# A first stage with an opening written out for three pairs, V in four loads, and inverse sums and weights at other steps

## The chip, the cores and the metric

The kernel runs on one core of one Trainium2 chip. The metric is the device time of one execution in microseconds (us). The engines are TensorE (PE), VectorE (DVE), ScalarE (ACT), GpSimd (POOL) and SyncE (SP), which here issues nearly all DMA transfers.

## What is computed

Attention over 4 batches, 12 heads, 448 positions and 64 columns per head, then two dense layers with gates. The reference, cut:

```python
def rmsnorm(x, g):
    return x / np.sqrt(np.mean(x * x, axis=-1, keepdims=True) + 1e-06) * g
q_n, k_n = rmsnorm(q, g_q), rmsnorm(k, g_k)
scores = np.matmul(q_n, k_n.transpose(0, 1, 3, 2)) / np.sqrt(64)
scores = scores - np.max(scores, axis=-1, keepdims=True)
attn = np.exp(scores)
attn = attn / (np.sum(attn, axis=-1, keepdims=True) + 1e-09)
x = np.matmul(attn, v)                 # then to (1792, 768)
g = x @ w_gate                         # 768 x 1536
x = (g / (1 + np.exp(-g)) * (x @ w_val)) @ w_out
h = x @ w2_in                          # 768 x 2048
out = (h * np.cos(h)) @ w2_out         # (1792, 768)
```

## The kernel before

Two heads of a batch make a pair; there are 24 pairs, six to a batch, and 7 column blocks (`NS`) to a pair. The kernel has a first stage for the 12 pairs of batches 0 and 1 (`NC`), a second for the attention of batches 2 and 3 beside the first dense layers, and stages for the remaining dense layers. The change touches the first stage.

The first stage is a loop over steps `n`, 7 steps to a pair. A table of offsets (`OFF`, third entry, less `CSH` = 12) says at which step each part of a pair's preparation is written: the loads of k and q into `rqk` (35 steps ahead of the pair's step 0), squares on ACT (L349) and their sums on VectorE (`ss`, L350), a power on POOL that gives the inverse norms (`ri`, from `ss` and `half`), products of k with the gains (L363) and of k and q with `ri` (k on VectorE, L408; q on POOL), casts to f16 on ACT (L423, L437) and the low halves on POOL (`h16`, L429 and L443), and a DMA transpose of `h16` into `T` (`c_T`, 18 steps ahead). The loop runs from step -35 on, and all of this goes through the table.

Of a pair's `T`, VectorE makes two copies (`c_copy`, L666 and L667) and ACT one, into the constant tile `cC`. `c_s` (12 steps ahead) makes scores on TensorE and takes each block's row maxima on VectorE (`sm`, L680). `c_row` puts the 7 maxima into the constant tile `cw` (L687, L688) and has TensorE turn them into rows by 7 small matmuls (`s<-id,cw`). `c_st` then makes transposed scores less their maxima, with `T` and `cC` as weights, and ACT's exponential (`pr`, L713). `c_av` multiplies with V: the tile `cV` holds V of a head beside ones, so that the same matmul gives outputs and sums. `c_x` copies the outputs out (`co`, L741). The sums go by DMA into a small tile (`c_sum`, `sm<-co`), are inverted (`c_inv`, L752, L753), written to DRAM (`c_out`, `rc<-sm`) and read back over 64 partitions each (`c_back`, `cr<-rc`); `c_mul` multiplies (L774), `c_lo` makes a low half. `CEND` holds the steps of these seven behind `c_x`. `v_max`, `v_row` and `v_out` find the largest element of V of a batch for a scale: two loads of V, two reductions, a matmul with the identity, small rows on VectorE, and a second matmul.

The constants of `cC`, `cw` and `cV` are set once per buffer by `c_const` on POOL (three buffers, the second and third at steps `CC1` and `CC2`).

Weights come as 64-bit numbers. `WSTEP` says at which steps of the first stage a piece is loaded (`raw`), converted to f32 by three rows on VectorE (L936 to L938) and squared on ACT, and split in two f16 halves (L968 on ACT, L969 on VectorE) that are also stored to DRAM (`scr_...`).

In this stage SP's and POOL's instructions stay in the order in which the code is written; TensorE's do so from step 75 (`EARLY`) on. For the others a scheduler sets the order when the kernel is built. Every engine runs its own list in order, so a row that waits holds all behind it. Operations on SP, POOL and TensorE pass a helper and have its line, L163.

Of the kernel before, what the change touches and what calls it, by code (L numbers as in the profile page):

```python
# [9 lines left out]
F32 = mybir.dt.float32  # L10
# [17 lines left out]
VM0 = 22  # L28
VM1 = 2
# [8 lines left out]
CXL = 11  # L38
VM2 = 46
CC1 = 22  # L40
CC2 = 29
# [8 lines left out]
for _u in range(WAHEAD):  # L50
    for _d, _w in ((-6, ("load", 0)), (-3, ("load", 1)), (0, ("conv", 0)), (4, ("conv", 1)), (7, ("scale", 1)), (8, ("split", 0)), (12, ("split", 1))):
        WSTEP.setdefault(8 + 16 * _u + _d, []).append((_w[0], 2 * _u + _w[1]))
# [119 lines left out]
def kernel(ctx: ExitStack, tc, q, k, v, g_q, g_k, w_gate, w_val, w_out, w2_in, w2_out, out):  # L172
# [84 lines left out]
    def emit_consts(gtmp):  # L257
        sync.dma_start(gk, g_k.partition_broadcast(P))
        sync.dma_start(gtmp, g_q.partition_broadcast(P))
        nc.vector.memset(half, -0.5)  # L260
        nc.vector.memset(hpi, math.pi / 2)
        make_identity(nc, ident)
# [139 lines left out]
    def p_mul(g):  # L402
# [4 lines left out]
        if "qm" in cf:  # L407
# [17 lines left out]
    def p_klo(g):  # L425
        pg = prep[g]
        k3, h16 = pg["rqk"][:, 1], pg["h16"]
        eng = gps if "kl" in cfg(g) else nc.vector
# [200 lines left out]
    def c_const(i):  # L629

        C = ctile("C", [P, NS, P], F16)
        gps.memset(C[HP:], 0.0)
        for r in (HP, HP + 32):
            gps.memset(C[r:r + 1], -(2.0 ** 14))
        W = ctile("w", [P, NS, HP], F16)
        gps.memset(W, 0.0)
        if i < 2:
            V = ctile("V", [P, 4, 2, P], F32)
            gps.memset(V[:, :, 0, HP:], 1.0)
            gps.memset(V[:, :, 1, :HP], 1.0)  # L640
            colv[i] = V
# [55 lines left out]
    def c_st(n):  # L697
# [17 lines left out]
    def c_av(g, j):  # L715
# [3 lines left out]
        for h in range(2):  # L719
# [3 lines left out]
            pe.matmul(pg["o"][h][:, :S], colv[g % 2][rows, j, h], e[rows], start=(j == 0), stop=(j == 3))  # L723
# [920 lines left out]
```

## Time and profile before

| | us |
|---|---|
| median of 3 runs | 1267.55 (1262.73 to 1267.83) |
| the profiled execution | 1267.07 |
| its span | 1265.3 |
| TensorE busy | 1171.3 (93%) |
| VectorE busy | 962.1 (76%) |
| ACT busy | 688.5 (54%) |
| POOL busy | 380.9 (30%) |

Busy shares are means over stages with different limits, so the stretches of the first stage (until about 228 us) are read one by one. In a timeline a line has its start, its length, the engine, the source line, what it writes and reads, and in brackets how long the engine had stood idle and what ended that. DMA lines of SP give the time of issue; landing is later. PEclk is TensorE's granted clock as a share of 2.4 GHz, so 0.50 is its level of 1.2 GHz.

### The profile page before, as it was taken

The numbers are of one execution on the slowest core, as the hardware profiler recorded it, in microseconds if no ns is written. First come the engines' busy times: TensorE is split into PE (matmuls) and PEld (weight loads), VectorE is DVE, ScalarE is ACT, GpSimd is POOL, SyncE is SP. The second block draws the span as 40 slices with busy tenths as digits, with TensorE's granted clock in tenths as the row PEclk, the third lists the DMA queues.
The fourth block names the chain that finished last, engine by engine and source line by source line (L and its number), as shares of the span: only waits on it lengthen the run. The fifth ranks groups of instructions, "written<-read, shape, count | busy, mean of one in ns | idle before, by whom it ended". The sixth has DMA issues, their size and how long they took to land. (4 is left out here: it accounts for less than half of the span.)

```text
span 1265.3 us, 18148 instructions
## 1 busy us (share of the span) xinstructions
PE 1171.3 (93%) x6292; PEld 658.6 (52%) x6292; DVE 962.1 (76%) x1824; ACT 688.5 (54%) x1317; POOL 380.9 (30%) x309
## 2 busy tenths in 40 slices
PE   1798788998989998999999999999999999999998
PEld 0333333453765445944458654775555554666655
DVE  5987876789778998258863499747888788999882
ACT  3676655554466552455664247447667767666220
POOL 7644412435421354224554111521221121100000
PEclk9999889998999999999999999999999999999999
DMA  5645666567777878689857688771522245132122
GB/s 150 185 127 133 166 163 209 96 168 209 212 215 217 208 235 244 213 190 210 190 129 222 235 291 304 239 244 66 195 80 68 74 159 195 57 106 76 51 69 88
DMA packets 220780, 211.53 MB, mean 167 GB/s; under 512 B 147600, under 2 KB 178192, under 8 KB 220688
## 3 DMA queue, kind: packets, MB, share of 16 engines
q1 hardware_dynamic: 220688, 210.38, 57.5%
q8 instruction: 49, 0.80, 0.3%
q14 instruction: 43, 0.35, 0.1%
HBM read 138.44 MB, written 41.57 MB: 142 GB/s over the span
## 5 line engine op out<-in xcount | busy, mean ns | idle before, releaser
L163 PE MATMUL mm<-xy,wp 128*128 128x448 f16 x2484 | 493.5, 355 | 5.4 <-ACT co L735 2.5
L163 PEld LDWEIGHTS <-wp 128*128 128x128 f16 x2880 | 278.3, 99 | 279.6 <-issue 36.0
L163 PE MATMUL mm<-g,wp 128*128 128x448 f32 x864 | 183.6, 370 | 1.7 <-DVE ga L1142 1.7
L163 PEld LDWEIGHTS mm<-g,wp 128*128 128x128 f32 x864 | 161.1, 189 | 19.8 <-issue 4.7
L163 PEld LDWEIGHTS <-g 128*128 128x128 f16 x840 | 82.1, 98 | 55.3 <-DVE tmp L163 0.8
L163 POOL TENSOR_TENSOR g<-ga,g 128x448 fp32r<-128x448 f32 x48 | 64.8, 1364 | 146.1 <-ACT g L1144 145.8
L163 POOL TENSOR_TENSOR g<-tmp,g 128x224 f16<-128x224 f32 x64 | 47.8, 750 | 197.9 <-ACT g L1261 197.6
L508 ACT ACTIVATE pr<-s,sm,esc 128x448 f32<-128x448 f32 x84 | 60.3, 719 | 78.0 <-DVE sm L502 70.6
L163 PE MATMUL s<-T 128*64 128x448 f16 x336 | 63.9, 397 | 40.7 <-DVE T L667 22.9
L163 POOL TENSOR_TENSOR wp<-w,wp 128x768 fp32r<-128x768 f32 x36 | 70.2, 1954 | 58.3 <-ACT wp L1025 38.9
L163 PEld LDWEIGHTS <-T 128*64 128x64 f16 (+1 forms) x432 | 28.6, 109 | 111.1 <-issue 82.7
L936 DVE TENSOR_SCALAR w<-raw 128x768 int32<-128x768 int32 x68 | 47.0, 694 | 49.8 <-POOL wp L163 16.7
L498 DVE TENSOR_REDUCE sm<-s 128x1 f32<-128x448 f32 x84 | 51.1, 614 | 35.4 <-PE s L163 35.3
L163 POOL TENSOR_TENSOR ri<-ss,half 128x14 f32<-128x14 f32 x24 | 64.4, 2685 | 39.4 <-DVE ss L357 29.7
L938 DVE SCALAR_TENSOR_TENSOR w<-raw,w 128x768 int32<-128x768 int32 x68 | 73.9, 1088 | 0.6
L937 DVE SCALAR_TENSOR_TENSOR w<-raw,w 128x768 int32<-128x768 int32 x68 | 73.3, 1081 | 0.6
L956 ACT ACTIVATE raw<-w 128x768 f32<-128x768 f32 x56 | 47.0, 839 | 45.0 <-DVE w L938 31.6
L163 POOL TENSOR_TENSOR p<-pr,p 128x448 f16<-128x448 f32 x36 | 42.0, 1172 | 88.7 <-ACT p L532 69.8
L1254 ACT ACTIVATE tmp<-tmp 128x448 f32<-128x448 f32 x64 | 36.4, 571 | 49.8 <-DVE tmp L1253 48.5
L163 PE MATMUL mm<-wp,g 128*128 128x384 f16 x360 | 62.1, 326 | 0.5 <-DVE tmp L163 0.4
L713 ACT ACTIVATE pr<-c,esc 128x448 f32<-128x448 f32 x84 | 50.4, 629 | 21.3 <-PE c L163 21.2
L163 PE MATMUL s<-wp,g 128*128 128x384 f16 x360 | 61.9, 326 | 0.0
(201 smaller groups left out, 2017.8 us busy)
## 6 DMA issues: line engine op xcount, KB each, us to landing
raw<-in_moe_w_out_dram SPq DMA_DIRECT2D x28, 768.0 KB, 5.2
raw<-in_moe_w_in_dram SPq DMA_DIRECT2D x16, 768.0 KB, 5.6
raw<-in_moe_w_gate_dram SPq DMA_DIRECT2D x12, 768.0 KB, 6.1
raw<-in_moe_w_val_dram SPq DMA_DIRECT2D x12, 768.0 KB, 5.9
wp<-scr_gate SPq DMA_DIRECT2D x24, 384.0 KB, 4.4
w<-scr_out SPq DMA_DIRECT2D x24, 384.0 KB, 4.0
wp<-scr_val SPq DMA_DIRECT2D x24, 384.0 KB, 5.3
y<-tmp SPq DMA_DIRECT2D x30, 224.0 KB, 3.9
```

Of the source, the lines that this page charges most:

```text
L163: r = f(*args, **kw)
L498: nc.vector.tensor_reduce(sm[:, 0, t:t + 1], slot[n][:, :S], axis=AX.X, op=ALU.max)
L508: nc.scalar.activation(e, slot.pop(n)[:, :S], AF.Exp, bias=sm[:, 1, t:t + 1], scale=esc, accum_out=sm[:, 2, t:t + 1],)
L713: nc.scalar.activation(e, ps[:, :S], AF.Exp, scale=esc)
L936: nc.vector.tensor_scalar(wi, hi, 3, 0x3FFFFFF8, op0=ALU.logical_shift_left, op1=ALU.bitwise_and)
L937: nc.vector.scalar_tensor_tensor(wi, hi, -0x40000000, wi, op0=ALU.bitwise_and, op1=ALU.bitwise_or)
L938: nc.vector.scalar_tensor_tensor(wi, lo, 29, wi, op0=ALU.logical_shift_right, op1=ALU.bitwise_or)
L956: nc.scalar.activation(sq_dst[0], w32, AF.Square, accum_out=n[:, 0:1])
L1254: nc.scalar.activation(r, r, AF.Abs)
```

## The change

The first three pairs (`NBEGIN`) leave the table and get an opening of their own: their loads first; then V of pairs 0 and 1, the constants, squares and powers of all three; then products, casts and low halves pair by pair. For pairs 0 and 1 (`NFAST`) both products and both low halves are on VectorE, and their transposes follow directly. `g_k` and `g_q` are loaded from ACT's queue, where a first ACTIVATE on a constant also loads the table early. Of the three sets of `cC` and `cw`, POOL sets one and VectorE two. The loop starts at step -14. V lies as V of one head, ones, V of the other, and comes in four loads instead of five; the odd head's blocks change place in `c_st` and `c_av` to suit. `c_out`, `c_back`, `c_mul` and `c_lo` stand 1, 2, 2 and 2 steps later. Weight loads stand at 9 and 5 steps ahead of a unit's first conversion, formerly 6 and 3. `v_max` of batch 0 and 1 moves.

```diff
-VM0 = 22
-VM1 = 2
+VM0 = -2
+VM1 = 29
+NFAST = 2
+NBEGIN = 3
-CXL = 11
+CXL = 13
-CC1 = 22
-CC2 = 29
...
-    for _d, _w in ((-6, ("load", 0)), (-3, ("load", 1)), (0, ("conv", 0)), ...
+    for _d, _w in ((-9, ("load", 0)), (-5, ("load", 1)), (0, ("conv", 0)), ...
...
     def emit_consts(gtmp):
-        sync.dma_start(gk, g_k.partition_broadcast(P))
-        sync.dma_start(gtmp, g_q.partition_broadcast(P))
+        nc.scalar.dma_start(gk, g_k.partition_broadcast(P))
+        nc.scalar.dma_start(gtmp, g_q.partition_broadcast(P))
         nc.vector.memset(half, -0.5)
         nc.vector.memset(hpi, math.pi / 2)
+        nc.scalar.activation(osc[:, :1], hpi, AF.Square)
...
-        if "qm" in cf:
+        if g < NFAST:
+            for j in (1, 0):
+                nc.vector.tensor_tensor(
+                    rqk[:, j], rqk[:, j], ri[:, j].unsqueeze(2).to_broadcast([P, NS, D]), op=ALU.mult
+                )
+        elif "qm" in cf:
...
-        eng = gps if "kl" in cfg(g) else nc.vector
+        eng = gps if "kl" in cfg(g) and g >= NFAST else nc.vector
...
-        eng = gps if "ql" in cfg(g) else nc.vector
+        eng = gps if "ql" in cfg(g) and g >= NFAST else nc.vector
...
-    def c_const(i):
-
+    def c_const(i, eng):
         C = ctile("C", [P, NS, P], F16)
-        gps.memset(C[HP:], 0.0)
+        eng.memset(C[HP:], 0.0)
         for r in (HP, HP + 32):
-            gps.memset(C[r:r + 1], -(2.0 ** 14))
+            eng.memset(C[r:r + 1], -(2.0 ** 14))
         W = ctile("w", [P, NS, HP], F16)
-        gps.memset(W, 0.0)
...
+    def c_ones(i):
+        V = colv[i] = ctile("V", [P, 4, 3, D], F32)
+        gps.memset(V[:, :, 1], 1.0)
...
-            sync.dma_start(V[:HP, :4 - h, h, hs], src[:, 0:NS - h:2])
-            sync.dma_start(V[HP:, :3, h, hs], src[:, 1:NS:2])
-            if h:
-                sync.dma_start(V[HP:, 3, h, hs], src[:, NS - 1])
+            one, two = ((slice(0, HP), slice(HP, P)), (slice(HP, P), slice(0, HP)))[h]
+            sync.dma_start(V[one, :, 2 * h], src[:, 0::2])
+            sync.dma_start(V[two, h:3 + h, 2 * h], src[:, 1::2])
...
-    CEND = ((c_x, 0), (c_sum, 1), (c_inv, 3), (c_out, 4), (c_back, 6), (c_mul, 8), (c_lo, CXL))
+    CEND = ((c_x, 0), (c_sum, 1), (c_inv, 3), (c_out, 5), (c_back, 8), (c_mul, 10), (c_lo, CXL))
...
-    step(-LEAD, 0)
+    p_load(0)
     emit_consts(gtmp)
-    c_const(0)
+    for g in range(1, NBEGIN):
+        p_load(g)
+    for i in range(2):
+        c_ones(i)
+        c_v(i)
+    c_const(0, gps)
+    for i in (1, 2):
+        c_const(i, nc.vector)
+    for g in range(NBEGIN):
+        p_sq(g, 1)
+        p_sq(g, 0)
+        if g == 0:
+            emit_gains(gtmp)
+        p_pow(g)
+    for g in range(NBEGIN):
+        p_mul(g)
+        p_khi(g)
+        p_qhi(g)
+        p_klo(g)
+        p_qlo(g)
+        if g < NFAST:
+            c_T(g)
...
-    for n in range(1 - LEAD, NCB + CXX + CXL + 1):
+    for n in range(NBEGIN * NS - LEAD, NCB + CXX + CXL + 1):
```

Three places of the new order. First VectorE at the very start, behind the memsets of `half` and `hpi`. `ss` are sums of squares, `gk` and `gtmp` the two gains, `ri` (later) the inverse norms. Before:

```order
L350 TENSOR_REDUCE ss<-sq 128x7
L274 TENSOR_TENSOR gk<-gk,gtmp 128x64
L350 TENSOR_REDUCE ss<-sq 128x7
L275 TENSOR_REDUCE gmax<-gk 128x1
L357 TENSOR_SCALAR ss<-ss 128x14
```

Now, in the same place:

```order
L637 MEMSET cC 64x448 x2
L275 TENSOR_TENSOR gk<-gk,gtmp 128x64
L351 TENSOR_REDUCE ss<-sq 128x7
L639 MEMSET cC 1x896 x2
L641 MEMSET cw 128x224 x2
L639 MEMSET cC 1x896 x2
L351 TENSOR_REDUCE ss<-sq 128x7
L276 TENSOR_REDUCE gmax<-gk 128x1
L351 TENSOR_REDUCE ss<-sq 128x7
L358 TENSOR_SCALAR ss<-ss 128x14
```

Eight memsets came in, six of them between the two sums of pair 0, and the product of the gains stands ahead of the first sum.

Second, VectorE where the first powers come back, from the products with `ri` to the first copy of a `T`. Before (pair 0 is `rqk_241`, pair 1 `rqk_283`):

```order
L408 TENSOR_TENSOR rqk_241<-rqk_241,ri_288 128x448
L357 TENSOR_SCALAR ss_320<-ss_320 128x14
L408 TENSOR_TENSOR rqk_283<-rqk_283,ri_310 128x448
L666 COPY cB_333<-T_318 64x896
L667 COPY T_318<-T_318 64x896
```

Now (pair 0 `rqk_241`, pair 1 `rqk_261`, pair 2 `rqk_265`):

```order
L410 TENSOR_TENSOR rqk_241<-rqk_241,ri_314 128x448 x2
L435 TENSOR_TENSOR h16_341<-rqk_241,h16_341 128x7x64
L410 TENSOR_TENSOR rqk_261<-rqk_261,ri_325 128x448 x2
L449 TENSOR_TENSOR h16_341<-rqk_241,h16_341 128x7x64
L435 TENSOR_TENSOR h16_350<-rqk_261,h16_350 128x7x64
L449 TENSOR_TENSOR h16_350<-rqk_261,h16_350 128x7x64
L414 TENSOR_TENSOR rqk_265<-rqk_265,ri_336 128x448
L668 COPY cB_368<-T_346 64x896
L669 COPY T_346<-T_346 64x896
```

The q products and four low halves came in, and pair 1's products stand ahead of the last low half of pair 0 (`h16_341`, L449), which its transpose needs.

Third, the second unit of gate weights. SP's queue before, from the transpose of pair 7 on:

```order
L163 DMA_TRANSPOSE T_1175<-h16_987 128x14x128
L163 DMA rc3_1219<-sm_1152 128x7
L163 DMA scr_val_0_0_117<-wp_1211 128x1536
L163 DMA raw_1248<-in_moe_w_gate_dram 128x3x512
L163 DMA cr_1257<-rc3_1219 64x448 x2
L163 DMA rqk_1264<-in_k_dram 64x448 x2
```

SP's queue now, from the read-back of pair 2's inverse sums and the transpose of pair 7 on:

```order
L163 DMA cr_1132<-rc2_1054 64x448 x2
L163 DMA_TRANSPOSE T_1150<-h16_957 128x14x128
L163 DMA raw_1160<-in_moe_w_gate_dram 128x3x512
L163 DMA scr_val_0_0_117<-wp_1193 128x1536
L163 DMA rc3_1223<-sm_1129 128x7
L163 DMA rqk_1241<-in_k_dram 64x448 x2
```

The gate load moved ahead of the write of pair 3's inverse sums (`rc3`), and their read-back (`cr<-rc3`) went behind the next loads. On VectorE the first conversion row of this piece stood behind the `cw` rows of pair 6 before:

```order
L680 TENSOR_REDUCE sm_1160<-s_1282 128x1
L667 COPY T_1175<-T_1175 64x896
L687 TENSOR_SCALAR cw_264<-sm_1160 128x7
L688 SCALAR_TENSOR_TENSOR cw_264<-sm_1160,cw_264 128x7
L936 TENSOR_SCALAR w32_1385<-raw_1248 128x768
```

Now, on VectorE:

```order
L668 COPY cB_1246<-T_1150 64x896
L682 TENSOR_REDUCE sm_1135<-s_1176 128x1
L951 TENSOR_SCALAR winv_102<-nm_1155 128x1
L669 COPY T_1150<-T_1150 64x896
L952 RECIPROCAL wsc_103<-winv_102 128x1
L1143 TENSOR_SCALAR gs_2308<-winv_102,vsc_104,gs_2308 128x1
L940 TENSOR_SCALAR w32_1374<-raw_1160 128x768
L682 TENSOR_REDUCE sm_1135<-s_1201 128x1
L941 SCALAR_TENSOR_TENSOR w32_1374<-raw_1160,w32_1374 128x768
```

The conversion row (L940) went ahead of four maxima of pair 6 (`sm_1135`; the first of the four is shown), two splits of weights, a product and the `cw` rows of that pair.

## Rows read from the trace of the kernel before

**Rows 1.** Stretches: length, busy us of PE, PEld, DVE, ACT, POOL (instructions), PEclk, DMA share, GB/s.

```profile
39.50:108.00 68.50, 60.84 (x264) 24.68 (x261) 60.11 (x119) 48.53 (x90) 36.99 (x26) 0.98 0.62 165
120.50:134.00 13.50, 5.17 (x27) 2.20 (x26) 6.98 (x10) 4.32 (x9) 3.40 (x3) 0.84 0.71 196
227.70:1265.30 1037.60, 1005.42 (x5592) 591.04 (x5591) 792.23 (x1470) 555.06 (x1076) 281.44 (x220) 0.99 0.57 168
```

**Rows 2.** Timeline of VectorE in the opening.

```profile
7.71 0.23 DVE L274 TENSOR_TENSOR gk<-gk,gtmp 128x64 f32<-128x64 f32 x1 [0.79 <-DMA gtmp<-in_g_q_dram]
...
10.90 1.14 DVE L350 TENSOR_REDUCE ss<-sq 128x7 f32<-128x448 f32 x2
...
26.46 1.55 DVE L374 TENSOR_REDUCE vm<-raw 128x1 f32<-128x1344 f32 x1 [0.51 <-DMA raw<-in_v_dram]
...
36.85 0.17 DVE L688 SCALAR_TENSOR_TENSOR cw<-sm,cw 128x7 f16<-128x7 f32 x1
```

**Rows 3.** Timeline of ACT and POOL in the opening.

```profile
4.39 1.28 ACT L349 ACT_TABLE_LOAD   x1 [4.39 <-DMA rqk<-in_k_dram]
...
8.76 2.61 POOL L163 TENSOR_TENSOR ri<-ss,half 128x14 f32<-128x14 f32 x1 [2.15 <-DVE ss L357]
...
14.04 0.58 ACT L423 ACTIVATE h<-rqk 128x448 f16<-128x448 f32 x1 [1.04 <-DVE rqk L408]
14.69 2.02 POOL L163 TENSOR_TENSOR h<-rqk,h 128x448 f16<-128x448 f32 x2 [2.30 <-ACT h L423]
```

**Rows 4.** Timeline of SP's queue: time of issue.

```profile
3.11 0.43 SPq L163 DMA_DIRECT2D gtmp<-in_g_q_dram  x1
...
16.74 1.65 SPq L163 DMA_TRANSPOSE T<-h  x1
...
36.94 1.56 SPq L163 DMA_TRANSPOSE T<-h  x1
...
106.51 3.28 SPq L163 DMA_DIRECT2D cV<-in_v_dram  x5
```

**Rows 5.** Timeline of TensorE: first matmul, V's maximum, row matmuls of pair 0.

```profile
21.75 1.33 PE L163 MATMUL s<-T 128*64 128x448 f16 x6 [21.75 <-DVE T L667]
...
38.70 0.55 PE L163 MATMUL s<-vrow,full 1*128 1x2 f32 x2 [2.83 <-DVE vrow L386]
...
39.56 0.95 PE L163 MATMUL s<-id,cw 128*64 128x128 f16 x7
```

**Rows 6.** Tiles cC (until 60 us) and T (until 80 us): ns min/median/max.

```profile
L163 POOL MEMSET cC<- x9: 837/839/841, 3.0 to 38.7; 1x896 f16 x6, 64x896 f16 x3
...
L666 DVE COPY cB<-T x5: 389/390/756, 20.9 to 66.4; 64x896 f16<-64x896 f16 x5
...
DMA to landing us min/median/max: 4.0/4.1/7.4
```

**Rows 7.** Timeline around the second unit of gate weights, and a stretch behind it.

```profile
111.16 1.55 SPq L163 DMA_TRANSPOSE T<-h  x1
...
119.51 1.57 SPq L163 DMA_DIRECT2D raw<-in_moe_w_gate_dram  x1
...
126.95 0.56 DVE L936 TENSOR_SCALAR w<-raw 128x768 int32<-128x768 int32 x1 [6.46 <-DMA raw<-in_moe_w_gate_dram]
...
133.65 1.01 PE L163 MATMUL s<-id,cw 128*64 128x128 f16 x7 [8.33 <-DVE sm L680]
...
133.65:140.00 6.35, 6.09 (x21) 2.16 (x21) 5.34 (x12) 4.06 (x7) 4.54 (x3) 0.50 0.67 178
```

**Rows 8.** Waits of VectorE, 40 to 228 us: total, times, longest.

```profile
DVE w L936 <- DMA raw<-in_moe_w_val_dram: 4.8, 4, 2.2
DVE tmp L774 <- DMA cr<-rc: 4.4, 4, 1.5
```

**Rows 9.** Waits of SP's queue, 40 to 228 us.

```profile
SPq L163 <- DMA rc<-sm: 27.5, 11, 5.1
```

**Rows 10.** Waits of TensorE, 39.5 to 227.8 us.

```profile
PE s L163 <- DVE sm L680: 14.5, 10, 8.3
```

More of the change, by code (lines that the diff above doesn't have):

```diff
@@ L50 @@
 for _u in range(WAHEAD):
-    for _d, _w in ((-6, ("load", 0)), (-3, ("load", 1)), (0, ("conv", 0)), (4, ("conv", 1)), (7, ("scale", 1)), (8, ("split", 0)), (12, ("split", 1))):
+    for _d, _w in ((-9, ("load", 0)), (-5, ("load", 1)), (0, ("conv", 0)), (4, ("conv", 1)), (7, ("scale", 1)), (8, ("split", 0)), (12, ("split", 1))):
         WSTEP.setdefault(8 + 16 * _u + _d, []).append((_w[0], 2 * _u + _w[1]))
@@ L627, in ctile @@
         return c_p.tile(shape, dt, tag="c" + nm, name="c" + nm, bufs=COL[nm])
-    def c_const(i):
+    def c_const(i, eng):
         C = ctile("C", [P, NS, P], F16)
-        gps.memset(C[HP:], 0.0)
+        eng.memset(C[HP:], 0.0)
         for r in (HP, HP + 32):
-            gps.memset(C[r:r + 1], -(2.0 ** 14))
+            eng.memset(C[r:r + 1], -(2.0 ** 14))
         W = ctile("w", [P, NS, HP], F16)
-        gps.memset(W, 0.0)
[L637 to L641, printed above, removed]
+        eng.memset(W, 0.0)
         colc[i] = (C, W)
+    def c_ones(i):
+        V = colv[i] = ctile("V", [P, 4, 3, D], F32)
+        gps.memset(V[:, :, 1], 1.0)
     colv = {}
@@ L707, in c_st @@
                 rows = hs if h0 is None else slice(0, P)
-                k0 = (off + 2 * j) * P + h
-                w = wt.rearrange("p t q -> p (t q)")[:, k0:min(k0 + 2 * P - 1, (off + NS) * P):2]
+                t = (2 * j + h if j < 3 else NS - 1) if h0 is not None or h == 0 else 0
+                k0 = (off + t) * P + h
+                w = wt.rearrange("p t q -> p (t q)")[:, k0:k0 + (2 * P if h0 is not None else P) - 1:2]
                 pe.matmul(
@@ L722, in c_av @@
             e = col[g, 2 * j + h] if j < 3 else col[g, NS - 1]
-            pe.matmul(pg["o"][h][:, :S], colv[g % 2][rows, j, h], e[rows], start=(j == 0), stop=(j == 3))
+            w = colv[g % 2][rows, (j + h) % 4, h:h + 2].rearrange("p k d -> p (k d)")
+            pe.matmul(pg["o"][h][:, :S], w, e[rows], start=(j == 0), stop=(j == 3))
     def c_x(g):
@@ L821, in s_prep @@
             for g in range(NPAIR):
-                if NS * g + OFF[ph(g)][nm] - (CSH if g < NC else 0) == n:
+                if g >= begun.get(nm, 0) and NS * g + OFF[ph(g)][nm] - (CSH if g < NC else 0) == n:
                     if g < NC and nm in ("vhi", "vlo"):
@@ L1408 @@
     in_order.update(("SP", "POOL"))
-    step(-LEAD, 0)
+    p_load(0)
     emit_consts(gtmp)
-    c_const(0)
+    for g in range(1, NBEGIN):
[20 more added lines that the diff above has]
+            c_T(g)
+    begun = {"load": NBEGIN, "vload": 2, "sqk": NBEGIN, "sqq": NBEGIN, "pow": NBEGIN, "mul": NBEGIN,
+             "khi": NBEGIN, "klo": NBEGIN, "qhi": NBEGIN, "qlo": NBEGIN, "T": NFAST}
     def w_step(n):
@@ L1417 @@
     cur = {}
-    for n in range(1 - LEAD, NCB + CXX + CXL + 1):
+    for n in range(NBEGIN * NS - LEAD, NCB + CXX + CXL + 1):
         for f, at in ((v_max, 0), (v_row, VMR), (v_out, VMO)):
-            for b, vn in enumerate((VM0 - LEAD, VM1, VM2)):
+            for b, vn in enumerate((VM0, VM1, VM2)):
                 if n == vn + at:
                     f(b)
-        if n == 2 - LEAD:
-            emit_gains(gtmp)
-        if n in (CC1 - LEAD, CC2 - LEAD):
-            c_const(1 if n == CC1 - LEAD else 2)
         if n == EARLY:
```

1 line of the change is left out of this document (removed).

## The prediction

> **What bounds the kernel now.** I read the table of stretches first. Behind 227.7 us TensorE is busy 1005.42 of 1037.60 us [rows 1], and the change leaves the order of the engines there as it was, but for some rows in the first part of it. So a microsecond won in the first stage should reach the end, and the question is only how long the first stage is. It has three parts. Until 39.56, where the row matmuls of pair 0 start [rows 5], TensorE has nearly nothing to do. From 39.5 to 108 VectorE is busy 60.11 of 68.50 us and TensorE 60.84 [rows 1]: VectorE's order sets the pace, and each of its waits costs. From 120.5 to 134 TensorE is busy only 5.17 of 13.50 us [rows 1].
>
> That hole is the largest single loss, and the timeline gives its cause [rows 7]: the load of gate weights was issued at 119.51, VectorE stood 6.46 us at its first conversion row until it had landed (126.95, so 7.4 us after its issue), and TensorE waited 8.33 us for row maxima queued behind that row. It then ran at a granted clock of 0.50 (the level of 1.2 GHz) from 133.65 to 140, busy 6.09 of 6.35 us [rows 7]; at the full level half of that, 3.0 us, would have done. The list of VectorE's waits in 40 to 228 adds 4.8 us for the loads of val weights and 4.4 us for the inverse sums [rows 8]; SP's queue stands 27.5 us waiting for its own writes of inverse sums before it may read them back [rows 9].
>
> **The opening.** Before, the transpose of pair 0 was issued at 16.74, TensorE began at 21.75, and the last row that the row matmuls need (L688) was at 36.85; the row matmuls came at 39.56, since TensorE's queue holds the matmul of V's maximum in front of them (38.70) [rows 2, 4, 5]. Walk through the new order of VectorE with the durations of before:
>
> Gain and product of gains: gtmp was issued at 3.11 [rows 4] and used at 7.71 [rows 2], 4.6 us later. On ACT's queue it can go at about 1.2, so this row, now ahead of the first sum of squares, runs at about 5.8 to 6.0. The first sum takes 0.57 (two in 1.14, [rows 2]; I use 0.56 for every wide row): 6.6. Then come the constants: four memsets of one partition by 896 and two of 128x224. No row shows such a memset on VectorE. The nearest are POOL's memsets of cC, 0.84 each in the same shapes, and as lower end VectorE's copy of 896 f16 columns, 0.39 [rows 6]; I take 0.84, the row with the same operation, and 0.21 for 224 columns in proportion: 4 x 0.84 + 2 x 0.21 = 3.8, until 10.4. Two more sums, a maximum and the scaling make 1.4: 11.8. The first power starts there and not at 8.76 [rows 3], 3 us later. It takes 2.6, the second one until 17.1. Meanwhile VectorE has three sums, three products with the gain (6 x 0.56) and small rows (0.7) in its queue: 15.9. Then pair 0's two products (17.0), one low half (17.6; ACT's cast, 0.58 [rows 3], fits beside it), pair 1's two products (18.7), and only then pair 0's last low half: 19.3. So the first transpose goes at 19.3, **2.6 us later** than before, although the power's queue is shorter. Low halves on POOL, two in 2.02 [rows 3], would have been slower by 0.9, but pair 1's rows stand in between.
>
> It lands 4.1 us later [rows 6], at 23.4. From there to the last L690 VectorE has 16 wide rows (10 maxima, 4 sums, 2 products), 9.0 us, 6 copies at 0.35, one reduction of V at 1.55 [rows 2] and small rows (0.5): 13.2, and I add 1.2 for waits on the second transpose and the loads: 37.8. No V matmul stands ahead of the row matmuls any more, so they start at 38.0 and not 39.56: **1.5 us won**. With memsets at 0.39 it would be 3.3; with the longest landing of a transpose, 7.4 [rows 6], 1.8 lost. The third transpose goes at about 26, against 36.94 [rows 4]; that lead fills no gap by itself, since VectorE, not a late T, sets the pace up to 108.
>
> The Trainium skill has a rule against this part. On its page "VectorE: DVE Perf Modes", section "Zero memsets can be issued as uint32 (trn2)", a memset takes one cycle per element whatever the type, and only zeros can be issued at half the count. An estimate from that page of the Trainium skill is 0.93 us for each of the four rows of 896, and the sum would be 0.4 us worse. No run here shows it yet.
>
> V's four loads in place of five save one issue, 0.66 of 3.28 us of SP per pair [rows 4]; SP isn't the bound where TensorE and VectorE are busy, so zero, and the V matmuls keep number and size. The table load of ACT (1.28 at 4.39 [rows 3]) moves into idle time; hidden too, since the gain row above ends later than the first square. The V maximum of batch 1 (two rows of 1.55 [rows 2]) moves from the crowded stretch before 108 to one near its end: zero in sum.
>
> **Weights sooner.** The gate load now stands directly behind a transpose (issued 111.16, 1.55 long), so at about 112.7 and not 119.51 [rows 7], and lands at 120.1 if it takes 7.4 again. But VectorE's conversion row moves up too: four maxima, a product, two splits of weights and the two cw rows that stood ahead of it are now behind it, some 5 us, so its turn comes at about 115.5 to 118 and not 120.5. Of 6.46 us of wait 2 to 4.6 stay; I take 2.5, since the transpose's copies ahead of it are late themselves. That takes 4.0 from the gap of 8.33, and I take half of the 3.0 us of slow clock: **5.5 us won** (ends: 1 and 11.3). For the val loads, 4.8 us of waits with TensorE gaps of a similar size behind them, I take 1.5 (0 to 4.8).
>
> **Inverse sums later.** SP no longer waits between writing and reading back, since the next loads and V's four transfers (4 x 0.66 = 2.6 us of issue by [rows 4], and three loads) now lie between. But the read-back now stands behind the next pair's sums, which wait for ACT's copies. VectorE's 4.4 us of waits for it [rows 8] are the price; half goes, 2.0 with what earlier transposes give (0 to 4.4; a loss of up to 2 if ACT's copy is late).
>
> **Sum.** 1.5 + 5.5 + 1.5 + 2.0 = 10.5. The profiled execution took 1267.07 us (span 1265.3), 0.5 below the median of 1267.55. 1267.07 - 10.5 = **1256.6**; own range of this case 1252 to 1262.
>
> **Rivals.** First, everything pays: memsets at 0.39 (3.3), TensorE's waits for maxima from 39.5 to 227.7 all gone (14.5, the 8.33 in it [rows 10]), and no slow clock behind them (3.0): 20.8, so 1246.3. For it: third and later transposes are some 10 us ahead. Against it: 88% of VectorE is used already.
>
> Second, the wait moves with the conversion: the load lands late at its new turn too, because the transpose ahead of it on SP waits for POOL's low halves. Then the weights give 1 and the read-back 1, with the opening's 1.5: 1263.5. For it: load and conversion both moved up by about the same 4 to 7 us.
>
> Third, slower: VectorE pays for what it took over. Eight memsets (3.8, and 0.42 for each of 64x448: 4.6 us), four low halves (2.2) and two products (1.1) are 8 us more of VectorE's rows before the same L690. I hide all of them in the idle time ahead of the first transpose's landing. If the loads, V's transfers and two transposes in a row land late (7.4 in place of 4.1), the first chain restarts behind them and the 8 us show: 1267.1 + 8 - 1 = 1274. It decides if the first L690 is later than 36.85 + 8 = 45.
>
> **How the numbers follow.** Forecast 43%, everything pays 20%, the wait moves 25%, slower 12%. A measurement of this kernel can tell some 0.5% (6.3 us) from no change, so faster means below 1261.2 and slower above 1273.9. Faster: nearly all of the forecast (0.38), the first rival (0.20) and a little of the second (0.02), 0.60. Same: most of the second and the rest of the forecast, with the milder end of the third, 0.29. Slower 0.11. The range goes from the first rival's value to just above the second's: 1246 to 1268; outside lie the third and what lies below the first.
>
> **What would show it.** Right: first transpose on SP at 18 to 21, first row matmuls at 37 to 39, no TensorE gap above 5 us from 40 to 215, the first stage's end near 217 in place of 227.7. Wrong: one-partition memsets well under 0.5 us, a first transpose before 16 (then the first rival), a conversion row on VectorE that waits over 5 us for gate weights (second), the first L690 behind 45 (third), or stretches behind 227.7 that lose what the first stage won.

## The result, and the profile after

The changed kernel takes 1269.97 us in the median of 20 runs (1266.34 to 1279.64); the kernel before, on the same chip, 1264.20 in 20 runs. The ratio is 1.0051, with a 95% interval of 1.0038 to 1.0065: slower by half a per cent, where 10.5 us less was forecast. The profiled execution took 1272.58, 2.6 above that median. Ratios, here and below, leave out runs that lie over 1.5% above the fastest of their kernel, such as one of w_only's at 3707.68.

The stretches of one execution, cut at the first row matmul of pair 0 and at the first block of second-stage matmuls (columns as in [rows 1]). Before:

```profile
39.56:227.70 188.14, 158.96 (x675) 65.36 (x673) 145.74 (x298) 121.80 (x222) 70.90 (x51) 0.94 0.62 169
```

After:

```profile
41.05:232.79 191.74, 163.44 (x677) 66.75 (x678) 151.33 (x309) 121.80 (x222) 71.77 (x48) 0.91 0.60 161
232.79:1270.50 1037.71, 1004.17 (x5592) 589.23 (x5591) 788.66 (x1465) 555.28 (x1075) 281.27 (x218) 0.99 0.57 168
```

Behind the first stage nothing changed: 1037.71 against 1037.60 [rows 1]. The loss is in the first stage: it starts 1.49 us later (41.05 against 39.56 [rows 5]) and its body, from there to its end, is 3.60 us longer (191.74 against 188.14), where 179.1 was forecast. TensorE's idle time in the body is almost what it was, 191.74 - 163.44 = 28.3 against 29.2, although the hole of 8.33 us is gone.

The opening of VectorE after, by its timeline (answers to [rows 2]):

```profile
6.55 0.23 DVE L275 TENSOR_TENSOR gk<-gk,gtmp 128x64 f32<-128x64 f32 x1 [4.61 <-DMA gtmp<-in_g_q_dram]
7.53 0.62 DVE L351 TENSOR_REDUCE ss<-sq 128x7 f32<-128x448 f32 x1 [0.75 <-ACT sq L350]
8.38 0.81 DVE L639 MEMSET cC<- 1x896 f16 x1 [0.24 <-DVE ss L351]
9.41 0.81 DVE L639 MEMSET cC<- 1x896 f16 x1 [0.22 <-issue]
10.31 0.49 DVE L641 MEMSET cw<- 128x224 uint32 x2
...
12.05 0.81 DVE L639 MEMSET cC<- 1x896 f16 x1 [0.22 <-issue]
12.89 0.62 DVE L351 TENSOR_REDUCE ss<-sq 128x7 f32<-128x448 f32 x1
...
20.39 1.16 DVE L410 TENSOR_TENSOR rqk<-rqk,ri 128x448 f32<-128x448 f32 x2 [0.58 <-POOL ri L163]
...
38.64 1.54 DVE L375 TENSOR_REDUCE vm<-raw 128x1 f32<-128x1344 f32 x1
...
40.71 0.19 DVE L690 SCALAR_TENSOR_TENSOR cw<-sm,cw 128x7 f16<-128x7 f32 x1
```

The same opening on the other engines, then the longest TensorE gap between 42 and 200 us and the place of the old hole (answers to [rows 3, 4, 5, 7]):

```profile
6.92 1.06 ACT L350 ACTIVATE sq<-rqk 128x448 f32<-128x448 f32 x2 [3.81 <-DMA rqk<-in_k_dram]
14.32 8.58 POOL L163 TENSOR_TENSOR ri<-ss,half 128x14 f32<-128x14 f32 x3 [7.51 <-DVE gmax L277]
22.12 3.83 SPq L163 DMA_TRANSPOSE T<-h  x2
30.25 1.74 SPq L163 DMA_TRANSPOSE T<-h  x1
41.05 0.61 PE L163 MATMUL s<-id,cw 128*64 128x128 f16 x4 [5.04 <-DVE cw L690]
...
53.70 0.76 DVE L940 TENSOR_SCALAR w<-raw 128x768 int32<-128x768 int32 x1 [2.02 <-DMA raw<-in_moe_w_gate_dram]
60.93 0.47 PE L163 MATMUL s<-T 128*64 128x448 f16 x2 [2.83 <-DVE sm L682]
...
111.53 1.13 SPq L163 DMA_DIRECT2D raw<-in_moe_w_gate_dram  x1
117.16 1.03 DVE L940 TENSOR_SCALAR w<-raw 128x768 int32<-128x768 int32 x1
...
124.28 0.43 SPq L163 DMA_DIRECT2D raw<-in_moe_w_gate_dram  x1
131.00 0.56 DVE L940 TENSOR_SCALAR w<-raw 128x768 int32<-128x768 int32 x1 [0.16 <-DMA raw<-in_moe_w_gate_dram]
```

Of the eight memsets that VectorE took over (sets 1 and 2), two ran at 1.03; the other six stand between the first and the second sum of pair 0, though VectorE had stood idle for 4.61 us just before. The power starts at 14.32 (8.76 before [rows 3]), the transpose at 22.12 (16.74 [rows 4]). The gate load is out at 111.53 (119.51 [rows 7]) and is converted at 117.16 without a wait, where VectorE stood 6.46 us before; the unit's second piece, out at 124.28, is converted at 131.00 after 0.16 us. A new wait of 2.02 for the first unit's second half stands at 53.70, with a TensorE gap behind it at 60.93.

TensorE's waits in the body, and SP's wait for its own writes, after (total, times, longest; answers to [rows 9, 10]):

```profile
PE s L163 <- DVE sm L682: 9.8, 8, 2.8
PE s L163 <- DVE cw L690: 8.0, 2, 5.0
PE u L163 <- ACT pr L716: 4.1, 1, 4.1
...
SPq L163 <- DMA rc<-sm: 2.3, 1, 2.3
```

The waits for maxima fell from 14.5 to 9.8 and SP's for its own writes from 27.5 to 2.3 as meant. Other waits of SP took their place: 22.9 us for splits of weights and 15.8 for TensorE. Of the 8.0 for L690, 5.0 end at 41.05 and lie ahead of the body; the other 3.0 end at 201.36, at the last pair. The 4.1 for exponentials end at 222.53; before, TensorE waited 2.2 for `cw` rows and 3.3 for exponentials, in pieces of at most 1.8.

One stretch must not be read as the kernel's: in the profiled execution TensorE, nearly idle from 36 to 41, ran at half clock from 34 to 46.

```profile
34.00:46.00 12.00, 6.13 (x23) 2.21 (x23) 11.87 (x24) 6.08 (x11) 5.25 (x4) 0.50 0.57 215
```

From 41 on that is 5 us of matmuls at half speed, so by estimate about 2.5 of this execution's time, which is also 2.6 above the median. Over the 20 runs the mean granted clock is 0.983, and 0.983 for the kernel before in 21 runs beside the first four experiments: no part of the 5.8 us is seen to come from the clock.

### The profile page after: what moved, and what is told of

The parts are those of the page before. It is cut to its first block, busy times and chain, and to the rows that moved or that the text cites. A ratio compares the mean times of both kernels' runs of the same rounds, so it can differ in the third digit from the quotient of the medians.

```text
span 1270.5 us, 18124 instructions
## 1 busy us (share of the span) xinstructions
PE 1173.2 (92%) x6292; PEld 657.7 (52%) x6292; DVE 969.9 (76%) x1838; ACT 690.8 (54%) x1318; POOL 373.8 (29%) x293
## 5 line engine op out<-in xcount | busy, mean ns | idle before, releaser
L940 DVE TENSOR_SCALAR w<-raw 128x768 int32<-128x768 int32 x68 | 50.6, 748 | 48.8 <-POOL wp L163 19.3
L960 ACT ACTIVATE raw<-w 128x768 f32<-128x768 f32 x56 | 47.0, 840 | 52.9 <-DVE w L942 39.4
L942 DVE SCALAR_TENSOR_TENSOR w<-raw,w 128x768 int32<-128x768 int32 x68 | 72.4, 1067 | 0.5
L941 DVE SCALAR_TENSOR_TENSOR w<-raw,w 128x768 int32<-128x768 int32 x68 | 72.2, 1065 | 0.6
L163 POOL TENSOR_TENSOR h<-rqk,h 128x448 f16<-128x448 f32 x32 | 38.5, 1207 | 92.7 <-ACT h L443 52.1
```

Of the source, the lines that this page charges most:

```text
L163: r = f(*args, **kw)
L940: nc.vector.tensor_scalar(wi, hi, 3, 0x3FFFFFF8, op0=ALU.logical_shift_left, op1=ALU.bitwise_and)
L941: nc.vector.scalar_tensor_tensor(wi, hi, -0x40000000, wi, op0=ALU.bitwise_and, op1=ALU.bitwise_or)
L942: nc.vector.scalar_tensor_tensor(wi, lo, 29, wi, op0=ALU.logical_shift_right, op1=ALU.bitwise_or)
L960: nc.scalar.activation(sq_dst[0], w32, AF.Square, accum_out=n[:, 0:1])
```

## The experiments

Each kernel was run beside the kernel before; "ratio" is to it, with its 95% interval. In brackets: first row matmul, and length of the body, of the profiled execution. 39.56 and 188.1 before, 41.05 and 191.7 after. Bodies come from single executions, so the ratios decide.

**Which part loses.** Four kernels: weights alone, inverse sums alone, the opening (with V's new layout) alone, and all but the opening.

```diff
# w_only: before, with
-((-6, ("load", 0)), (-3, ("load", 1)),
+((-9, ("load", 0)), (-5, ("load", 1)),
# inv_only: before, with
-(c_out, 4), (c_back, 6), (c_mul, 8)      CXL = 11
+(c_out, 5), (c_back, 8), (c_mul, 10)     CXL = 13
# open_only: after, with both undone
# no_open: before, with both and V in four loads
```

> The kernel before with one edit: the two weight loads of each unit go three and two steps sooner, nothing else. Theory A (the sooner load alone closes the hole at 120.5 to 134, and the loss of the changed kernel comes from its opening): VectorE's wait at the gate conversion of the second unit falls from 6.46 to under 2.5 us, TensorE's gap of 8.33 goes, and the time is 4 to 9 us below the kernel before, ratio 0.993 to 0.997. Rival B (the hole closes only because the new opening brings the transposes forward, or because every reshuffle of the order moves it): a wait over 4 us stays, and the ratio is 0.998 to 1.003.

> The kernel before with one edit: the inverse sums are written out, read back and used one and two steps later. Theory A: SP's 27.5 us of waits between writing and reading back fall under 5, the gain is 0 to 3 us (0.9975 to 1.000), since the read-back itself was waited for only 4.4 us by VectorE. Rival C (the later use delays the corrections at the end of the stage, where the changed kernel has gaps of 3.00 and 4.09 us): 1 to 4 us slower, ratio 1.001 to 1.003, with the gaps in the last 30 us of the first stage.

> The changed kernel with weights and inverse sums put back to their old steps: the new opening with its four V loads alone. Theory A (the opening is what costs): the row matmuls of pair 0 start at about 41 at the half clock as in the changed kernel, and with a hole for the gate weights still in it the time is 5 to 12 us above the kernel before, ratio 1.004 to 1.010. Rival B (the opening's lead closes the hole): no hole at 120 to 134, ratio 0.997 to 1.003.

> The kernel before with everything of the change but its opening: four V loads with the new layout, inverse sums later, weights sooner. Theory A: row matmuls at 39.5 and no hole at 120 to 134, 5 to 9 us below the kernel before, ratio 0.993 to 0.996. Rival B: ratio 0.998 to 1.003. Rival C (later inverse sums cost at the stage's end): it stands 1 to 4 us above the kernel that only has the weights sooner.

Measured: w_only 1.0067 [1.0044, 1.0091] (38.47, 194.2); inv_only 1.0004 [0.9990, 1.0018] (38.37, 190.4); open_only 1.0069 [1.0048, 1.0090] (40.41, 198.6); no_open 0.9983 [0.9969, 0.9998] (38.78, 185.1). The opening costs 8.6 us with the new steps (0.9983 to 1.0051), and with V's layout as much with the old ones (1.0069). Without it the rest gains 2 us, not 9. And sooner weights alone lose 8.5: the hole closed there too (the load was out at 110.45, and its conversion at 117.91 did not wait), but VectorE's waits for the read-back of the inverse sums went from 4.4 to 7.9 us. That these 3.5 us are the cause of the 8.5 is not shown. Theory A was right on the opening and wrong on the weights. Of rival C the sign in the last 30 us came (in inv_only TensorE waits 3.72 us for exponentials at 218.84), a loss in time is not clear (1.0004 [0.9990, 1.0018]).

**What in the opening.** The gains loaded on SP, the constants on POOL, and both.

```diff
# gains_sp: after, with
-nc.scalar.dma_start(gk, ...); nc.scalar.dma_start(gtmp, ...)
+sync.dma_start(gk, ...); sync.dma_start(gtmp, ...)
# const_pool: after, with c_const(1, ...) and c_const(2, ...) moved behind the three p_pow
-        c_const(i, nc.vector)
+        c_const(i, gps)
# both_fix: both
```

> The changed kernel with one edit: the two gain vectors are loaded on SP's queue behind the first pair's loads, as before, and not on ACT's at the same time. Theory D (the second queue delays pair 0's keys: the first square starts at 6.92 in the changed kernel against 5.69 before): the first square starts at 5.7 or earlier, the first power 1 to 2 us sooner, first row matmuls at 39 to 40, time 1 to 2.5 us below the changed kernel, ratio to the kernel before 1.003 to 1.0045. Rival E (the memsets between the sums set the first power, and the product of gains just waits longer): first square sooner, first power unmoved within 0.7 us, ratio 1.004 to 1.0065 as the changed kernel.

> The changed kernel with one edit: the constants of sets 1 and 2 (cC, cw) are written by POOL behind its three powers and not by VectorE. Theory E (eight memsets between pair 0's sums, some 4.7 us with their gaps, are what made the opening late, and what the opening loses at pair 0 the kernel keeps to the end): first power at 9.5 to 10.5 in place of 14.32, first transpose on SP at 17 to 18.5 in place of 22.12, first row matmuls at 35 to 38 in place of 41.05, time 4 to 7 us below the changed kernel, ratio 0.9965 to 1.002. Rival F (VectorE's rows of all pairs and not the first chain set the pace): the opening is earlier by the same amount, but the time stays within 2 us of the changed kernel, ratio over 1.0035.

> Both edits: constants of sets 1 and 2 on POOL, gains loaded on SP behind the first pair. Theory D with E: first power at 8.3 to 9, first transpose at 15.5 to 17.5, row matmuls at 33.5 to 37, and 1 to 2 us below the kernel with the constants on POOL alone. Rival: the second edit adds nothing, within 1 us.

Measured: gains_sp 1.0050 [1.0030, 1.0070] (40.73, 195.3); const_pool **0.9929** [0.9902, 0.9955] (33.17, 182.9), median 1257.25; both_fix 0.9934 [0.9914, 0.9955] (33.00, 186.1). Rows of gains_sp, ACT and POOL:

```profile
4.37 1.12 ACT L350 ACTIVATE sq<-rqk 128x448 f32<-128x448 f32 x2 [2.16 <-DMA rqk<-in_k_dram]
13.98 8.65 POOL L163 TENSOR_TENSOR ri<-ss,half 128x14 f32<-128x14 f32 x3 [7.16 <-DVE ss L358]
```

The keys were there 2.5 us sooner and the power started only 0.3 sooner, since all six memsets still stood ahead of pair 0's scaling row (L358 at 13.73): rival E, not theory D. In both_fix, too, the second edit adds nothing. Rows of const_pool, POOL, SP and TensorE:

```profile
9.30 2.96 POOL L163 TENSOR_TENSOR ri<-ss,half 128x14 f32<-128x14 f32 x1 [2.48 <-DVE ss L358]
15.41 3.90 SPq L163 DMA_TRANSPOSE T<-h  x2
29.16 1.54 SPq L163 DMA_TRANSPOSE T<-h  x1
33.17 0.61 PE L163 MATMUL s<-id,cw 128*64 128x128 f16 x4 [2.93 <-DVE ss L358]
```

Everything in the first chain is 5 to 8 us sooner, rather more than theory E said. But the gain is 1.2%, some 15 us, twice the opening's lead of 7.9 and twice what theory E allowed. Half of it had no explanation.

**Place of the memsets, and the two steps on the new opening.** const_first leaves the memsets on VectorE but runs them before the first sum, where VectorE waits anyway.

```diff
# const_first: after, with VectorE in written order from the memsets to the product of gains
+    in_order.add("DVE")
     for i in (1, 2):
-        c_const(i, nc.vector)
+        c_const(i, vec)
# fix_oldw, fix_oldinv: const_pool with the old weight steps, or the old CEND and CXL
```

> The changed kernel with its eight memsets kept on VectorE, but put ahead of the first sum, into the time from 1.0 to 6.5 us in which VectorE waits for the gains; nothing leaves VectorE. Theory E (it is their place in pair 0's chain that costs): first power at 8.5 to 10.5, first transpose at 16.5 to 18.5, and the time falls with it, by 5 to 12 us against the changed kernel (ratio to the kernel before 0.995 to 1.001). Rival G (VectorE has too many rows, wherever they stand, and POOL has to take them): ratio over 1.002. What separates it from the kernel with the constants on POOL is then the order behind the opening, above all the two rows of V's maximum (1.54 each) that still stand ahead of L690.

> The kernel with the constants on POOL, with the weight loads put back to their old steps. My prediction's term (the sooner weights are worth 7.0 us): 1262 to 1266, 5 to 9 above the kernel with the constants on POOL. Rival (the two step changes together gave only 2.3 us with the old opening and 3.7 with the new one, so the weights are worth little): within 3 us of it.

> The kernel with the constants on POOL, with the inverse sums put back to their old steps. My prediction's term (2.0 us): 1258 to 1261. Rival (sooner weights without later inverse sums lost 8.5 us with the old opening, so the two belong together): 5 to 9 us above the kernel with the constants on POOL, with VectorE waiting over 7 us for the read-back of the inverse sums. Third: no difference within 1.5 us.

Measured: const_first 1.0015 [1.0000, 1.0030] (36.45, 192.8); fix_oldw 1.0006 [0.9991, 1.0022] (33.20, 199.1); fix_oldinv 1.0022 [0.9999, 1.0044] (33.21, 193.6). The place of the memsets is worth 4.6 us (1.0051 to 1.0015), as much as the row matmuls come sooner (41.05 to 36.45); the time is just above theory E's range and just below rival G's. The step from there to const_pool, 0.9%, is something else. The weights' steps are worth 10 us here and the inverse sums' 12, where I had 7.0 and 2.0. Waits of VectorE and SP in fix_oldinv:

```profile
DVE tmp L778 <- DMA cr<-rc: 11.5, 8, 3.0
...
SPq L163 <- DMA rc<-sm: 20.9, 11, 4.3
```

With the old steps SP stands 20.9 us between writing and reading back, and what is queued behind it, the sooner weights too, waits along: the rival's sign, and more than its 5 to 9 us. The read-back alone (11.5) is about as much as the 12 us.

**V's maximum, and neither step.** In after and const_first one row of V's maximum (1.54) stands ahead of L690 and two stand ahead of pair 3's product.

```diff
# first_vm0: const_first, with
-VM0 = -2
+VM0 = 0
# fix_neither: const_pool with both old steps
```

> The kernel with the memsets ahead of the sums, with one more edit: the load and the two rows of V's maximum for batch 0 come two steps later (VM0 from -2 to 0), so that on VectorE they stand behind L690 of pair 0 and behind pair 3's product (L414), and not ahead. Theory H (in the changed kernel and in the one with the memsets first, these two rows of 1.54 hold up L690 by 2 us and pair 3's product by 3, with it the fourth transpose, the second gate load behind it on SP, and so TensorE's gap of 2 to 3 us at 56 to 61): row matmuls at 34 to 35 in place of 36.45, fourth transpose at 38.5 to 40 in place of 42.11, no gap over 2 us at 56 to 61, ratio to the kernel before 0.992 to 0.997. Rival I (the rest of the way to the kernel with the constants on POOL, 8 us or more, has nothing to do with these rows): ratio 0.9995 to 1.003 as before the edit.

> The kernel with the constants on POOL, with weights and inverse sums both put back to their old steps: the opening without its memsets, and four V loads, alone. If the opening's lead carries through by itself (row matmuls at 33.2 against 39.56 before): 4 to 7 us below the kernel before, ratio 0.9945 to 0.997. Rival J (the old steps cannot use the lead, since SP's queue is held up behind the inverse sums and the weights come late; with either one put back the ratio was 1.0006 and 1.0022): 0.9985 to 1.003, with VectorE waiting over 15 us in all for weights and read-back.

Measured: first_vm0 1.0004 [0.9985, 1.0023] (34.90, 194.2); fix_neither 1.0063 [1.0038, 1.0087] (32.95, 202.0). In first_vm0 every local sign came as forecast, row matmuls at 34.90, the fourth transpose at 39.52 and not 42.11, no gap of 2 us at 56 to 61, and the time hardly moved: theory H falls. fix_neither shows that with the old steps the opening's lead of 6.6 us is worth nothing: its body is 14 us longer than before's, and the time 0.6% above.

**Small edits, and work added.** Does any small edit move the time as much? And is it POOL's delay that helps in const_pool? first_again tests the second with work that is useless: POOL writes constants that VectorE has already written.

```diff
# pool_vm0: const_pool with VM0 = 0.   v4_only: before with V in four loads
# const_split: set 1 as in const_first, set 2 as in const_pool
# first_again: const_first, and behind the three p_pow
+    for i in (1, 2):
+        c_again(i)          # the memsets of c_const(i) once more, on gps
```

> The kernel with the constants on POOL, with one small edit that leaves its opening alone: V's maximum of batch 0 two steps later (VM0 from -2 to 0). Theory M (the constants off VectorE are worth their 10 us whatever the order behind them): ratio to the kernel before 0.991 to 0.996. Rival L (most of what lies beyond the opening's lead hangs on the exact order behind it, and any edit deals it anew): 0.997 to 1.003.

> The changed kernel with the constants of set 1 on VectorE in its idle time ahead of the first sum, and those of set 2 on POOL behind the powers. First row matmuls at 34 to 36.5. Theory M (VectorE's rows in idle time cost nothing, the opening's lead decides): between the kernel with the memsets first (1.0015) and that with the constants on POOL (0.9929), by its row matmuls, 0.994 to 0.999. Rival L: anywhere from 0.993 to 1.004, and not by the opening.

> The kernel before with one edit: V of the first stage in four loads instead of five, in the new layout. My prediction's term is zero, 0.999 to 1.001: SP saves 0.66 us per pair where it is not the bound. Rival L (any edit deals the order behind it anew): up to 5 us off to either side, 0.996 or 1.004, with no wait on V's transfers to show for it.

> The kernel with the memsets first on VectorE, and POOL writes the same constants once more behind its three powers, 6.6 us of POOL as in the kernel with the constants on POOL. Theory K (that kernel gains by what it delays: pair 2's third transpose, at 29.16 there and 24.92 with the memsets first, and what queues behind it on SP, come later and stand less in the way of pairs 0 and 1): third transpose at 28 to 30, ratio to the kernel before 0.992 to 0.997. Without it: 1.000 to 1.004, as with the memsets first.

Measured: pool_vm0 0.9960 [0.9942, 0.9977] (32.96, 181.4); const_split 1.0007 [0.9991, 1.0023] (36.70, 193.2); v4_only 1.0026 [1.0013, 1.0039] (38.84, 188.3); first_again **0.9945** [0.9926, 0.9965] (36.18, 182.8). Body of const_first, then of first_again, by the table of stretches:

```profile
36.45:229.20 192.75, 162.34 (x677) 66.45 (x678) 150.44 (x309) 121.77 (x222) 70.72 (x48) 0.93 0.58 160
```

```profile
36.18:218.95 182.77, 159.29 (x677) 64.80 (x678) 146.81 (x309) 120.54 (x221) 66.78 (x47) 0.94 0.66 176
```

With 6.6 us of useless POOL work the first stage ends 10 us sooner from almost the same start. Timeline rows of const_first (SP, VectorE, TensorE) and of first_again (SP):

```profile
24.92 2.23 SPq L163 DMA_TRANSPOSE T<-h  x1
49.48 1.39 DVE L940 TENSOR_SCALAR w<-raw 128x768 int32<-128x768 int32 x1 [2.38 <-DMA raw<-in_moe_w_gate_dram]
56.60 0.58 PE L163 MATMUL s<-T 128*64 128x448 f16 x2 [3.04 <-DVE sm L682]
```

```profile
30.34 1.55 SPq L163 DMA_TRANSPOSE T<-h  x1
```

The third transpose, of pair 2, comes 5.4 us later, and the wait for the gate half with TensorE's gap behind it, which after shows too (53.70, 60.93), is gone. VectorE's wait for the scale of V (`vsc`, L393) in 36 to 130 us goes with it, in const_first and then in first_again:

```profile
DVE vsc L393 <- PE s L163: 3.5, 1, 3.5
```

```profile
DVE vsc L393 <- PE s L163: 1.0, 1, 1.0
```

These waits all lie before 130 us, and most of the 10 us comes later, as the table by pairs below shows. const_split goes against theory M (VectorE's rows in idle time cost nothing): its opening leads as const_first's does and it gains no more. The two small edits moved the time by 0.3% each, v4_only's clear of noise, pool_vm0's (against const_pool) just at the edge of it: what rests on one order of rows alone is uncertain by about that much.

**The same delay in the changed kernel, and a later pair 2 without added work.**

```diff
# after_again: after with c_again as above.   first_nb2: const_first with
-NBEGIN = 3
+NBEGIN = 2
```

> The changed kernel itself, its memsets where they are, with POOL writing the same constants once more behind its three powers (6.6 us of POOL): work added, none taken away. Theory K (in the changed kernel, too, pair 2 comes to its transpose too soon behind pair 0, 8.1 us, and what is behind the opening pays some 9 us for it): third transpose at 33 to 37, first row matmuls within 1 us of 41, the stretch from them to the end of the first stage 183 to 187 us in place of 191.7, ratio to the kernel before 0.996 to 1.000. Rival (the delay helps only where the opening is early): 1.003 to 1.008.

> The kernel with the memsets first on VectorE, with two pairs in the opening in place of three (NBEGIN from 3 to 2), so that pair 2 is prepared in its step and its transpose comes later without any work added. Theory K: first row matmuls at 33 to 36.5, stretch behind them 180 to 186 us, ratio 0.990 to 0.995. Rival L (the order is dealt anew and the lead goes): 0.998 to 1.004.

Measured: after_again 0.9989 [0.9973, 1.0005] (40.40, 186.1); first_nb2 **0.9934** [0.9910, 0.9957] (30.42, 189.4), median 1258.67. Useless POOL work takes 0.6% off the changed kernel with its opening as late as it was. Its third transpose moved less than I expected (32.15, not 33 to 37). With two pairs in the opening the gain came with an opening 6 us sooner still; its body of 189.4 is not the 180 to 186 that theory K asked for. const_pool, both_fix and first_nb2 all beat both kernels, by 0.7% against the kernel before and 1.2% against the changed one.

**Where the time goes, by pairs.** The traces answer in part what the runs leave open. The body is cut at the row matmuls of pair 9; the next column counts the rows of weight conversion that stand on VectorE from 2 us ahead of pair 10's row matmuls up to the last pair's last `cw` row (each from one profiled execution).

| kernel | row matmuls of pair 0 | from there to pair 9's | from there to the end | conversion rows | ratio |
|---|---|---|---|---|---|
| before | 39.56 | 139.3 | 48.9 | 3 | 1 |
| no_open | 38.78 | 132.2 | 52.9 | 7 | 0.9983 |
| after | 41.05 | 134.0 | 57.7 | 9 | 1.0051 |
| after_again | 40.40 | 132.7 | 53.4 | 9 | 0.9989 |
| const_first | 36.45 | 137.4 | 55.4 | 9 | 1.0015 |
| first_again | 36.18 | 134.0 | 48.8 | 2 | 0.9945 |
| const_pool | 33.17 | 132.6 | 50.3 | 2 | 0.9929 |
| first_nb2 | 30.42 | 135.9 | 53.5 | 9 | 0.9934 |

So the changed kernel is 3.7 us ahead of the kernel before at pair 9 (175.09 against 178.82) and 5.1 behind at the end of the stage. Rows of VectorE, and TensorE's last line, in after; then VectorE in before and in first_again:

```profile
191.34 0.56 DVE L940 TENSOR_SCALAR w<-raw 128x768 int32<-128x768 int32 x1 [0.39 <-DMA raw<-in_moe_w_gate_dram]
...
196.92 1.82 DVE L941 SCALAR_TENSOR_TENSOR w<-raw,w 128x768 int32<-128x768 int32 x2
...
200.26 0.94 DVE L942 SCALAR_TENSOR_TENSOR w<-raw,w 128x768 int32<-128x768 int32 x1
201.13 0.18 DVE L690 SCALAR_TENSOR_TENSOR cw<-sm,cw 128x7 f16<-128x7 f32 x1
201.36 0.85 PE L163 MATMUL s<-id,cw 128*64 128x128 f16 x6 [3.00 <-DVE cw L690]
```

```profile
200.80 0.96 DVE L938 SCALAR_TENSOR_TENSOR w<-raw,w 128x768 int32<-128x768 int32 x1
201.67 1.02 DVE L688 SCALAR_TENSOR_TENSOR cw<-sm,cw 128x7 f16<-128x7 f32 x1
```

```profile
186.79 0.96 DVE L948 SCALAR_TENSOR_TENSOR w<-raw,w 128x768 int32<-128x768 int32 x1
187.67 0.18 DVE L697 SCALAR_TENSOR_TENSOR cw<-sm,cw 128x7 f16<-128x7 f32 x1
```

In after nine conversion rows, 7.2 us, stand ahead of that row, in before three, in first_again two. Kernels with two or three take 48.7 to 50.3 us from pair 9 to the end (pool_vm0 and both_fix have two as well, v4_only three), those with five or more 51 to 59. The same 176 matmuls there keep TensorE busy for 46.4 us in after and 41.9 in before, at a mean granted clock of 0.84 and 0.93. Between const_first and first_again 3.4 us are won up to pair 9 and 6.6 behind it. No run moves these rows alone, so that they are the cause is not shown; and why the scheduler puts them there with one edit and not with another stays open.

## Why the prediction was wrong, step by step

**The opening: -1.5 forecast, +1.5 at the first row matmul, 8.6 in the time.** The price of a memset was right: 0.81 for one partition by 896 where I took 0.84, 0.245 where I took 0.21. The Trainium skill's rule ("VectorE: DVE Perf Modes", "Zero memsets can be issued as uint32 (trn2)": one cycle per element whatever the type) agrees with the trace in proportion: 896 f16 took 0.81 and 448 uint32 0.43. Its rate does not: my estimate from the page was 0.93 for the 896. What failed is the sum ahead of the first transpose. The first sum ran at 7.53, not 6.0; 0.22 to 0.24 lies ahead of most memsets, so they last from 8.38 to 12.86, 4.5 and not 3.8; the power started at 14.32, not 11.8, and took 2.86 a piece. The transpose went at 22.12, not 19.3. From there to L690 I had 18.5, measured 18.6. So 2.8 us were lost before the first transpose and none behind it. That makes the row matmuls 3.05 us later than forecast (41.05, not 38.0), the smaller part of the 10.1 between my -1.5 and the 8.6. By the table 4.8 of the opening's cost (after less no_open) arise from pair 9 on. That the memsets' place is worth the 4.6 us that the row matmuls come sooner is in part chance: between after and const_first 3.3 us are lost up to pair 9 and 2.3 won behind it.

**"That lead fills no gap by itself": the term set to zero.** I saw the third transpose come early and priced it at nothing, because VectorE sets the pace up to 108. It came at 30.25, 6.7 us ahead of before; the fourth was 1.9 ahead (46.70), the fifth behind (60.55 against 60.03 before). With useless POOL work behind the powers the time falls 0.7% with the memsets first and 0.6%, 8 us, in the changed kernel itself, so what follows the opening is not free. But that the early third transpose is the cost, theory K, is not shown. It follows the first by 8.1 us in after and const_first and 10.2 in const_split (no faster than const_first), by 10.6 in after_again and 13.8 and 13.9 in const_pool and first_again (all faster); it follows by 13.8 in fix_oldw, fix_oldinv and fix_neither too, at 1.0006 to 1.0063. The scheduler lays out another order for each of these, no run separates that order from the delay, and two thirds of first_again's gain lie behind pair 9.

**Weights, -7.0: the mechanism was right, the step to the end was not.** The conversion at 117.16 waits for nothing, in place of 6.46, and behind the row matmuls no gap over 5 us is left, as forecast; VectorE's waits for val weights fell from 4.8 to 2.7. Up to pair 9 the body is 5.2 us shorter than before's, of the 9.0 forecast for weights and inverse sums. What failed is "a microsecond won in the first stage should reach the end": from pair 9 on the stage takes 8.8 us more (57.7 against 48.9), and I had no term for the last pairs, where the conversions now stand ahead of the last `cw` row. I also added this term to the next as if each stood alone. Ratios to the kernel before:

| opening | old steps | weights sooner | inverse sums later | both |
|---|---|---|---|---|
| before's | 1 | 1.0067 | 1.0004 | 0.9983 (with V in four) |
| new | 1.0069 | | | 1.0051 |
| new, constants on POOL | 1.0063 | 1.0022 | 1.0006 | 0.9929 |

In the changed kernel (second row) both steps together give 0.2%, 2.3 us of the 9.0. With before's opening weights alone lose 0.7% and both gain 0.2%; in the last row weights alone give 0.4%, inverse sums alone 0.6% and both 1.3%, a surplus over the sum that the intervals do not rule out as noise.

**Inverse sums, -2.0: undersized.** SP's 27.5 us of waits fell to 2.3, and I took only VectorE's 4.4 us as their price. Alone they are worth nothing (1.0004); beside sooner weights they are worth 0.8 to 0.9%, 11 us. That the price was what stood behind SP in its queue is likely and not shown.

**V in four loads, 0:** 0.26% slower, with no wait on V's transfers to show for it; the order behind it changed, the cause stays open.

**Rivals.** That everything pays: no, the first transpose was at 22.12, not before 16. That the wait moves with the conversion: no, there is none at 117.16. That VectorE pays for its new rows, 1274, from a first L690 later than 45: the time was near, the mechanism was not. L690 was at 40.71, and the memsets, put into VectorE's idle time, left 4.6 us less to pay. A slower case with another cause stood in none of my cases.

## What to carry to other kernels

Before rows are given to an engine with time to spare, look where its spare time lies and whether the new rows can run there: here six memsets stood between two sums of the first chain while VectorE had idled 4.6 us just before. Do not add gains that pass through the same in-order queues: measure them together and apart, since sooner loads alone lost 8.5 us and with later inverse sums they won. And follow a gain to the end of its stage: the changed kernel was 3.7 us ahead at pair 9 and 5.1 behind at the end, with six more conversion rows ahead of the last pair's row matmuls. Where a scheduler deals the order anew with each edit, look there before a gain or a loss is put down to the edit itself: 6.6 us of useless work made two kernels faster.

## What the runs showed of the hardware

Memsets cost by columns and not by partitions: on POOL 1x896 and 64x896 both take 0.84 us [rows 6], on VectorE 0.805 us for 1x896 f16, 0.432 for 64x448 and 0.245 for 128x224 as uint32. By an estimate from these three, 0.058 us and 0.833 ns per column. Some 0.22 us of idle time stood ahead of each 1x896. Two gain vectors loaded from ACT's queue, issued at 0.72 and 1.13 beside the first keys at 0.72, put off the first square, which waits for the keys, from 4.37 (gains_sp) to 6.92 (after); in both_fix and const_pool it is 3.92 and 6.59. The Trainium skill ("DMA: Bandwidth & Descriptors", "Issuing engines are not separate DMA queues") says that transfers started from several engines run on the same 16 DMA engines and interleave; the rows fit that, and show what it can cost the transfer that is waited for.
